# Token blocks of twice 460 or 462 columns instead of twice 384 in the middle and last stage of an attention and gated feed-forward kernel

## The chip, the cores and the metric

The kernel runs on one core of one Trainium2 chip. The time is that of one launch on the device, in microseconds (us). The profile names the engines of the core as PE (TensorE, the matrix engine), PEld (its weight loads, which overlap the matmuls), DVE (VectorE), ACT (ScalarE), POOL (GpSimd) and SP (SyncE, which issues all transfers here). Names such as L615 are lines of the kernel before.

## The reference

Sliding-window attention with a linear bias over 8 batches, 8 heads and 576 positions of width 64, and then a gated feed-forward layer over the 4608 tokens, 512 wide with 1536 hidden units:

```python
scores = scale * np.matmul(q, k.transpose(0, 1, 3, 2))
mask = (rel >= 0) & (rel < window)                       # window 128
scores = np.where(mask, scores + bias[None], -1000000000.0)
attn = softmax(scores)
x = np.matmul(attn, v) as (4608, 512)
gate = 1.0 / (1.0 + np.exp(-(x @ w_gate)))
val = x @ w_val
return (gate * val @ w_out)
```

## The kernel before

**Stages.** The first stage does the attention of 32 units (batch and pair of heads), writes x to DRAM (`xs`), and beside it `gates1` makes the hidden units of the first four chunks of 128 (`FC1`) for nine blocks of 512 tokens (L533). The middle stage, `gates2`, makes the other eight chunks of hidden units for six blocks of 768 tokens (L615), each block as two halves of N2 = 384 columns. The last stage, `results`, multiplies by `w_out` for the same six blocks (L728). Hidden units pass through DRAM in between (`hs`): `spill` stores them and `results` loads them again.

**Seven products.** Middle and last stage treat a block as a matrix of 2 x 2 parts (the two token halves by the two halves of the contraction) and form its product with the weights from seven products of sums and differences of the parts instead of eight of the parts themselves. `mix` (L659) and, in `results`, `add` (L699) form these sums on DVE; `parts` splits each into a high and a low part in a reduced format (ACT or DVE casts, L179 or L180; DVE subtracts, L188). Each product then takes three matmuls for every 128 rows of the contraction: high by high, high by low, low by high. One chunk of a block in the middle stage is 7 products x 2 x 3 = 42 matmuls of 384 columns, a block 336. A block of the last stage is 7 products x 2 output tiles x 6 pieces of the contraction x 3 = 252 matmuls of 384 columns. Each matmul has its own weights, so each has a weight load.

**Buffers.** The seven split sums of a block of the middle stage stand in three tiles, cxA (products 0, 3, 4), cxB (1, 5, 2) and cxC (6), which exist once: the next block's sum is written when the last chunk's product with the old one has been read. In the last stage the six rows of chunks of a product come in two pieces of HC = 3 chunks (1152 columns), split into seven places in turn: hF, which is memory of its own, two each in h0 and h1, which take over the memory of cxA and cxB, and two in h2, where the raw weights were. The weights of the last stage (wos0 to wos5) take over the memory of those of the middle stage (w2s0 to w2s5).

**Order.** Nothing is issued as the code is written: a planner (`Graph.order`) gives each operation a cost (for a group of matmuls, N / 2400 + 0.0133 us each) and lists them by the time at which it expects them to start. Each engine then runs its own list in order, with waits for what an operation reads. SP's queue is such a list too: loads of `xr` (x for the middle stage), `hq` and `hr` (hidden units), stores of `hs` and `out`. `follow` and `close` are entries without work that say which buffers take over which. `spill` cuts stores where a block of 512 tokens of the first stage crosses an edge between the later blocks.

## Time and profile before

| what | value |
|---|---|
| runs of before | 1019.53 us median of 3 (1019.47 to 1019.97) |
| the profiled execution | 1020.78 us, its span 1019.1 us |
| matmuls L533 / L615 / L728 | 864 / 2016 / 1512 |
| attention's last matmuls | about 303 us from the start |
| first matmul of the middle stage | 401.7 us |
| first matmul of the last stage | 751.5 us |
| last activation | 1015.2 us |

The profile is one execution. Its span is 1.7 us shorter than the time of that execution, and that time is 1.25 us above the median of the runs. A row of a group gives the number of instructions behind "x", then busy time in us and the mean duration in ns, then the idle time of the engine before them and what ended it. In the timeline a row is a run of like instructions: start, length, engine, line, operation, number. Matmuls overlap in the records: each is recorded with 334 ns while the next one starts about 173 ns later, so the spacing of starts says what a matmul costs, not its duration.

### The profile page before, as it was taken

To read this page: it belongs to the slowest core of one execution; us is meant where nothing else is said; L and a number is where in the kernel's file an instruction comes from. 1 tells how busy PE (TensorE), PEld (TensorE's weight loads), DVE (VectorE), ACT (ScalarE), POOL (GpSimd) and SP (SyncE) were. 2 spreads that over 40 slices of the span, in tenths; PEclk is the share of its full clock that TensorE was granted. 3 is DMA by queue.
4 is the path that set the end of the run, shared out by engine and by line. 5 is a ranking of instruction groups with operands and counts; after the bars stand their busy time and mean duration, and the time that the engine had idled before them with its cause. 6 is when DMAs were issued, how large, how long until landed. Compare 5 with 4: busy or idle time off the path is not lost.

```text
span 1019.1 us, 19617 instructions
## 1 busy us (share of the span) xinstructions
PE 1001.0 (98%) x7038; PEld 908.0 (89%) x7038; DVE 795.8 (78%) x2039; ACT 494.1 (48%) x1342; POOL 111.1 (11%) x211
## 2 busy tenths in 40 slices
PE   9899899999999999999999999999999999999998
PEld 7667677777777778999999999999999999999998
DVE  8999888888868887978473745547898988989881
ACT  6998777777864333454343433435364422212220
POOL 2333343333320000000000000000010000000000
PEclk9999899999999999999999999999999999999999
DMA  8776765646436554676231221313635364353401
GB/s 288 262 236 207 225 213 194 235 158 234 142 115 187 169 176 155 203 247 211 74 110 62 75 96 47 124 47 113 233 96 199 107 196 143 129 163 113 151 24 62
DMA packets 94129, 158.56 MB, mean 156 GB/s; under 512 B 8784, under 2 KB 69584, under 8 KB 94032
## 3 DMA queue, kind: packets, MB, share of 16 engines
q1 hardware_dynamic: 94032, 157.32, 46.8%
q8 instruction: 55, 0.90, 0.4%
q14 instruction: 42, 0.34, 0.1%
HBM read 106.95 MB, written 50.33 MB: 154 GB/s over the span
## 4 chain that ended last, share of the span: by engine, by line
PE 70%; DVE 15%; ACT 8%; issue 3%; DMA 3%; SPq 0%; ACTq 0%; DVEq 0%
PE mm L615 33%; PE mm L728 25%; PE mm L533 7%; ACT pb L390 5%; DVE mm L375 4%; DVE pb L387 2%; DVE work L273 2%; DVE pb L411 1%; DVE x L188 1%; ACT pb L410 1%; DVE st L405 1%; PE mm L415 1%; DMA work<-in_moe_w_val_dram 1%; PE mm L352 1%; DMA work<-in_moe_w_gate_dram 1%
## 5 line engine op out<-in xcount | busy, mean ns | idle before, releaser
L533 PE MATMUL mm<-x,w 128*128 128x512 f32 x864 | 222.9, 402 | 4.3 <-DVE x L188 3.1
L728 PE MATMUL mm<-h,wos 128*128 128x384 f32 x1296 | 226.9, 334 | 0.1
L728 PEld LDWEIGHTS mm<-h,wos 128*128 128x128 f32 x1296 | 224.8, 188 | 0.4 <-DVE h L188 0.4
L533 PEld LDWEIGHTS mm<-x,w 128*128 128x128 f32 x864 | 155.0, 188 | 45.4 <-issue 7.6
L390 ACT ACTIVATE pb<-pb,st 128x128 f32<-128x128 f32 x288 | 112.7, 394 | 39.6 <-DVE st L387 39.3
L426 POOL TENSOR_SCALAR_AFFINE_SELECT pt<-both 128x384 f32<-128x384 f32 x192 | 100.3, 546 | 193.1 <-ACT both L179 163.6
L615 PE MATMUL mm<-cxA,w2s 128*128 128x384 f32 x648 | 120.9, 334 | 0.0
L615 PE MATMUL mm<-cxB,w2s 128*128 128x384 f32 x648 | 119.6, 334 | 0.0
L615 PEld LDWEIGHTS mm<-cxA,w2s 128*128 128x128 f32 x648 | 113.2, 188 | 0.1
L615 PEld LDWEIGHTS mm<-cxB,w2s 128*128 128x128 f32 x648 | 113.0, 188 | 0.0
L622 DVE TENSOR_TENSOR mm<-mm,ring 128x384 f32<-128x384 f32 x96 | 53.7, 563 | 75.4 <-PE mm L615 72.5
L179 ACT COPY ring<-mm 128x384 f32<-128x384 f32 x144 | 69.0, 479 | 78.5 <-PE mm L615 74.9
L626 ACT ACTIVATE sg<-mm 128x384 f32<-128x384 f32 x96 | 47.2, 491 | 115.2 <-PE mm L615 65.1
L188 DVE TENSOR_TENSOR h<-hr,h 128x1152 fp32r<-128x1152 f32 x66 | 88.7, 1354 | 4.4 <-ACT h L179 1.2
L740 ACT ACTIVATE ring<-mm 128x384 f32<-128x384 f32 x48 | 23.6, 492 | 103.1 <-PE mm L728 103.1
L387 DVE CUSTOM_DVE_ANT_0 pb<-mm,relm 128x128 f32<-128x128 f32 x288 | 68.5, 285 | 1.7
L415 PE MATMUL mm<-ident,pb 128*128 128x128 f32 x288 | 52.8, 289 | 7.5 <-ACT both L179 4.1
L179 ACT CAST h<-hr 128x1152 fp32r<-128x1152 f32 x30 | 34.6, 1161 | 50.3 <-PE mm L728 31.2
L375 DVE COPY_PREDICATED mm<-swap,mm 64x128 f32<-64x128 int32 x216 | 55.2, 294 | 4.7 <-PE mm L362 1.2
L410 ACT ACTIVATE pb<-pb,st 128x128 f32<-128x128 f32 x157 | 54.0, 394 | 8.7 <-DVE st L407 8.5
L415 PEld LDWEIGHTS mm<-ident,pb 128*128 128x128 f32 x288 | 32.9, 141 | 27.9 <-ACT both L179 10.3
L187 POOL TENSOR_TENSOR work<-work 128x256 f32<-128x256 f32 x6 | 5.9, 992 | 446.8 <-ACT sg L626 429.9
(97 smaller groups left out, 1440.1 us busy)
## 6 DMA issues: line engine op xcount, KB each, us to landing
hs<-ring SPq DMA_DIRECT2D x120, 192.0 KB, 1.9
hr<-hs SPq DMA_DIRECT2D x36, 576.0 KB, 4.9
kr<-in_k_dram SPq DMA_DIRECT2D x31, 576.0 KB, 4.5
qr<-in_q_dram SPq DMA_DIRECT2D x31, 320.0 KB, 4.8
vr<-in_v_dram SPq DMA_DIRECT2D x32, 288.0 KB, 3.5
xs<-xt SPq DMA_DIRECT2D x32, 288.0 KB, 2.9
out_dram<-ring SPq DMA_DIRECT2D x48, 192.0 KB, 1.9
xr<-xs SPq DMA_DIRECT2D x10, 768.0 KB, 5.5
```

Source lines behind the costliest of these rows:

```text
L179: g.add("ACT", act_cost(n, psum), lambda: nc.scalar.copy(out(), src()), reads, writes, want, release=release, ways=[("DVE", dve_cost(n, ps ...
L188: g.add("DVE", dve_cost(n, psum, True), lambda: nc.vector.tensor_tensor(out(), a(), b(), op=ALU.subtract), reads, writes, want, port=not p ...
L375: g.add("DVE", dve_cost(2 * D, psum=True), lambda b=b, col=col, to=to, of=of: nc.vector.copy_predicated(sp[b][col, :, to:to + D], swap[col ...
L387: g.add("DVE", 0.21, lambda: nc.vector.tensor_tensor_reduce(pb()[:, e], sp[j // 2][:, j % 2, first:first + P], relm[u.p][:, w], op0=ALU.ad ...
L390: g.add("ACT", 0.39, lambda: nc.scalar.activation(pb()[:, e], pb()[:, e], AF.Exp, bias=st()[:, e:e + 1], scale=-1.0, accum_out=st()[:, 3 + ...
L410: g.add("ACT", 0.3, lambda args=args: nc.scalar.mul(*args()), [(kst, 6)], [(kpb, e)], want, ways=[("DVE", 0.16, True, lambda args=args: nc ...
L415: nc.tensor.transpose(tp[:, e], pb()[:, e], ident)
L426: nc.gpsimd.affine_select(pt(u)[:, f0:f0 + 2 * n - 1:2, :], both(), [[0, n], step], cmp, 0.0, base=0, channel_multiplier=mult)
L533: nc.tensor.matmul(mm[s], w1(kind, wi)[:, i, c * P:(c + 1) * P], x1(x)[:, c, :], start=(k == 0 and c == 0), stop=(k == 2 and c == KC - 1))
L615: nc.tensor.matmul(mm[b][:, 0:N2], w2t(i, wp)[:, wk, c * P:(c + 1) * P], combo(k, xp)[:, c], start=(start and c == 0 and j == 0), stop=(c ...
L622: g.add("DVE", dve_cost(N2, psum=True), lambda: nc.vector.tensor_tensor(o(), bk(b)(), a(), op=ALU.add), [("mm", b), *reads] if okeys else ...
L728: nc.tensor.matmul(mm[banks_[i]][:, 0:N2], wot(e * HC + c, wp)[:, k, i * P:(i + 1) * P], hcombo(s, xp)[:, c], start=(start and e == c == j ...
```

## The change

The 4608 tokens are cut into five blocks instead of six, each of two halves: two blocks with halves of 462 columns and three with halves of 460 (2 x 2 x 462 + 3 x 2 x 460 = 4608). A table of edges takes the place of multiples of 384 where stores and loads are cut. In the last stage a piece is two chunks instead of three (twice 462 columns, 924 in all), and there are nine places instead of seven: the seven sums' own places of the middle stage, one each, and two in the memory of the raw weights. hF is gone. cxA and cxC move from the general pool to the one that opens when the attention's memory is given back, so their first sums must wait for that.

```diff
-N2 = 384
-NT2 = NT // (2 * N2)
-HC = NFC // 4
-NRING, NRING1, NHC = 10, 4, 7
+HALVES = (462, 462, 460, 460, 460)
+N2, NT2 = max(HALVES), len(HALVES)
+EDGE = [2 * sum(HALVES[:b // 2]) + b % 2 * HALVES[b // 2] for b in range(2 * NT2)] + [NT]
+HC = NFC // 6
+NRING, NRING1, NHC = 10, 4, 9
...
-            b = a // N2
-            e = min((b + 1) * N2, t0 + n)
+            b = max(b for b in range(2 * NT2) if EDGE[b] <= a)
+            e = min(EDGE[b + 1], t0 + n)
...
-        return T(moe, f"c{grp}", [P, 1 if grp == "xC" else 3, 2, 2, N2], F32R, tag=grp)[:, j, part_]
+        return T(moe if grp == "xB" else pools["w2"], f"c{grp}", [P, 1 if grp == "xC" else 3, 2, 2, N2], F32R, tag=grp)[:, j, part_]
...
-        t0 = t * 2 * N2
+        N, t0 = HALVES[t], EDGE[2 * t]
...
-                            nc.tensor.matmul(mm[b][:, 0:N2], w2t(i, wp)[:, wk, c * P:(c + 1) * P], combo(k, xp)[:, c],
+                            nc.tensor.matmul(mm[b][:, 0:N], w2t(i, wp)[:, wk, c * P:(c + 1) * P], combo(k, xp)[:, c, 0:N],
...
     def hcombo(s, part_):
-        if s == 0:
-            return T(pools["w2"], "hF", [P, 2, HC, N2], F32R)[:, part_]
-        return T(moe, f"h{(s - 1) // 2}", [P, 2, 2, HC, N2], F32R, tag=("xA", "xB", "xW")[(s - 1) // 2])[:, (s - 1) % 2, part_]
+        if s < len(ORDER):
+            return combo(ORDER[s], part_)
+        return T(moe, "hw", [P, 2, 2, HC, N2], F32R, tag="xW")[:, s - len(ORDER), part_]
...
-            for e in range(2):
-                move(lambda h=h, k=k, e=e: hquad(h, k)[:, halves[e]], lambda h=h, k=k, e=e: hs[k][2 * t + h][halves[e]].rearrange("c p t -> p c t"),
+            for e in range(3):
+                move(lambda h=h, k=k, e=e: hquad(h, k)[:, third[e], 0:N], lambda h=h, k=k, e=e: hs[k][2 * t + h][third[e]].rearrange("c p t -> p c t"),
...
-        slots = {(k, e): (2 * n + e) % NHC for n, k in enumerate(ORDER) for e in range(2)}
-        m = HC * N2
+        slots = {(k, e): (3 * n + e) % NHC for n, k in enumerate(ORDER) for e in range(3)}
+        m = HC * N
...
-    g.add("PY", 0.0, close, [], touched + ["w2pool"], FIRST)
+    g.add("PY", 0.0, close, [], touched + ["w2pool"] + [k for c in (0, 3, 4, 6) for k in both_("xc", c)], FIRST)
...
-    for s0, ks in ((1, (0, 3, 4)), (3, (1, 5, 2))):
-        follow([k for c in ks for k in both_("xc", c)], both_("hc", s0) + both_("hc", s0 + 1))
-    follow([("wraw", s) for s in range(NRAW)] + [("wbits", s) for s in range(2)] + [("tt", j) for j in range(2)], both_("hc", 5) + both_("hc", 6))
+    for s0, c in enumerate(ORDER):
+        follow(both_("xc", c), both_("hc", s0))
+    follow([("wraw", s) for s in range(NRAW)] + [("wbits", s) for s in range(2)] + [("tt", j) for j in range(2)], both_("hc", 7) + both_("hc", 8))
```

The rest of the diff puts N for N2 where a width is meant. PE's list is the same as before up to the last two blocks of 512 tokens of the first stage; SP's differs earlier, in where stores are cut. Three places show how the lists differ later on. In the changed kernel some lines have moved by one (L616 is L615 of before, L189 is L188, L623 is L622, L631 is L630, L700 is L699); x6 stands for six matmuls in a row.

PE's list where the last stage begins, before. Groups from L615 belong to the last chunk of the middle stage, in which cxA, cxB and cxC are the split sums; groups from L728 belong to the first block of the last stage, hF and h0 being places of pieces and wos0 to wos5 the weights of the chunks:

```order
L615 MATMUL mm5_153<-cxA_4697,w2s5_4522 128x384 x6
L615 MATMUL mm7_155<-cxA_4697,w2s5_4522 128x384 x6
L615 MATMUL mm5_153<-cxA_4697,w2s5_4522 128x384 x6
L615 MATMUL mm6_154<-cxB_4801,w2s5_4522 128x384 x6
L615 MATMUL mm5_153<-cxB_4801,w2s5_4522 128x384 x6
L615 MATMUL mm7_155<-cxB_4801,w2s5_4522 128x384 x6
L728 MATMUL mm0_148<-hF_7238,wos0_7333 128x384 x3
L728 MATMUL mm0_148<-hF_7238,wos1_7411 128x384 x3
L728 MATMUL mm0_148<-hF_7238,wos2_7465 128x384 x3
L615 MATMUL mm5_153<-cxC_4719,w2s5_4522 128x384 x6
L728 MATMUL mm1_149<-hF_7238,wos0_7333 128x384 x3
```

The same place of the changed kernel:

```order
L616 MATMUL mm5_149<-cxA_4697,w2s5_4514 128x460 x6
L616 MATMUL mm7_151<-cxA_4697,w2s5_4514 128x460 x6
L616 MATMUL mm6_150<-cxB_4797,w2s5_4514 128x460 x6
L616 MATMUL mm5_149<-cxA_4697,w2s5_4514 128x460 x6
L616 MATMUL mm7_151<-cxB_4797,w2s5_4514 128x460 x6
L616 MATMUL mm5_149<-cxB_4797,w2s5_4514 128x460 x6
L728 MATMUL mm0_144<-cxA_4697,wos0_6881 128x462 x3
L728 MATMUL mm0_144<-cxA_4697,wos1_6952 128x462 x3
L728 MATMUL mm1_145<-cxA_4697,wos0_6881 128x462 x3
L728 MATMUL mm1_145<-cxA_4697,wos1_6952 128x462 x3
L616 MATMUL mm5_149<-cxC_4724,w2s5_4514 128x460 x6
L728 MATMUL mm0_144<-cxA_4697,wos2_7007 128x462 x3
```

The first piece of the last stage is read from cxA, in the place of the sum that the last chunk's first group has read just before, instead of from hF.

DVE's list at the same place, before. `hq0` and `hr` are the loaded hidden units, L188 rows into h0 finish a piece, L622 and L630 are work on the last chunk's results, and rows into wos5 finish the last weights:

```order
L622 TENSOR_TENSOR mm6_154<-mm6_154,ring_76 128x384
L622 TENSOR_TENSOR ring_76<-mm5_153,ring_76 128x384
L622 TENSOR_TENSOR mm7_155<-mm7_155,ring_76 128x384
L188 TENSOR_TENSOR h0_7619<-hq0_7202,h0_7619 128x1152
L630 SCALAR_TENSOR_TENSOR ring_76<-sg0_882,mm7_155 128x384
L188 TENSOR_TENSOR h0_7619<-hr_7280,h0_7619 128x1152
L630 SCALAR_TENSOR_TENSOR ring_76<-sg1_892,ring_76 128x384
L188 TENSOR_TENSOR wos5_7674<-work_193,wos5_7674 128x256
L188 TENSOR_TENSOR wos5_7674<-work_193,wos5_7674 128x1536
```

The same place of the changed kernel:

```order
L623 TENSOR_TENSOR mm6_150<-mm6_150,ring_76 128x460
L189 TENSOR_TENSOR cxA_4697<-hq0_6751,cxA_4697 128x924 x2
L623 TENSOR_TENSOR mm7_151<-mm7_151,ring_76 128x460
L189 TENSOR_TENSOR cxA_4697<-hq0_6751,cxA_4697 128x924
L623 TENSOR_TENSOR ring_76<-mm5_149,ring_76 128x460
L631 SCALAR_TENSOR_TENSOR ring_76<-sg0_878,mm7_151 128x460
L189 TENSOR_TENSOR cxB_4797<-hr_6817,cxB_4797 128x924 x3
L631 SCALAR_TENSOR_TENSOR ring_76<-sg1_888,ring_76 128x460
L189 TENSOR_TENSOR wos5_7229<-work_189,wos5_7229 128x256
L700 TENSOR_TENSOR hr_6817<-hr_6817,hq0_6751 128x924
L189 TENSOR_TENSOR wos5_7229<-work_189,wos5_7229 128x1536
```

Six pieces of 924 columns stand ahead of wos5's first row instead of two pieces of 1152.

PE's list where the second block of the middle stage ends and the third begins, before (w67 holds the weights of chunks 6 and 7, the last of a block, w2s0 and w2s1 those of chunks 0 and 1):

```order
L615 MATMUL mm7_155<-cxB_4801,w67_4787 128x384 x6
L615 MATMUL mm0_148<-cxA_4697,w2s0_4163 128x384 x6
L615 MATMUL mm5_153<-cxC_4719,w67_4787 128x384 x6
L615 MATMUL mm2_150<-cxA_4697,w2s0_4163 128x384 x6
L615 MATMUL mm0_148<-cxA_4697,w2s0_4163 128x384 x6
L615 MATMUL mm1_149<-cxB_4801,w2s0_4163 128x384 x6
L615 MATMUL mm3_151<-cxA_4697,w2s1_4215 128x384 x6
L615 MATMUL mm2_150<-cxB_4801,w2s0_4163 128x384 x6
```

The same place of the changed kernel, where the new block's first row (of 460 columns) follows the old block's last one:

```order
L616 MATMUL mm7_151<-cxB_4797,w67_4783 128x462 x6
L616 MATMUL mm5_149<-cxC_4724,w67_4783 128x462 x6
L616 MATMUL mm0_144<-cxA_4697,w2s0_4159 128x460 x6
L616 MATMUL mm2_146<-cxA_4697,w2s0_4159 128x460 x6
L616 MATMUL mm0_144<-cxA_4697,w2s0_4159 128x460 x6
L616 MATMUL mm1_145<-cxB_4797,w2s0_4159 128x460 x6
L616 MATMUL mm3_147<-cxA_4697,w2s1_4211 128x460 x6
L616 MATMUL mm5_149<-cxA_4697,w2s1_4211 128x460 x6
L616 MATMUL mm2_146<-cxB_4797,w2s0_4159 128x460 x6
```

The new block's second cxB group now comes two groups of cxA later instead of one, with the old block's cxC ahead of all of them.

More of the change, by code (lines that the diff above doesn't have):

```diff
@@ L226, in attention_gated_ffn @@
     xs = [dram.tile([KC, P, S], F32, name=f"xs{b}") for b in range(B)]
-    hs = [[dram.tile([NFC // 2, P, N2], F32, name=f"hs{k}_{b}") for b in range(NT // N2)] for k in range(2)]
+    hs = [[dram.tile([NFC // 2, P, HALVES[b // 2]], F32, name=f"hs{k}_{b}") for b in range(2 * NT2)] for k in range(2)]
     wod = [dram.tile([P, DM], F32, name=f"wod{f}") for f in range(NFC)]
@@ L606, in chunk @@
             sa, su, sp_ = scratch(), scratch(), scratch()
-            a1, u2, p5 = (lambda s=s: ring2(s) for s in (sa, su, sp_))
-            sg = [lambda h=h: sgate(h)[:, 0:N2] for h in range(2)]
-            bk = lambda b: (lambda: mm[b][:, 0:N2])
+            a1, u2, p5 = (lambda s=s: ring2(s)[:, 0:N] for s in (sa, su, sp_))
+            sg = [lambda h=h: sgate(h)[:, 0:N] for h in range(2)]
+            bk = lambda b: (lambda: mm[b][:, 0:N])
             def product(k, b, start, wk):
@@ L619, in product @@
                       [("mm", b)], 1.0e6)
             def total(o, b, a, reads, writes, okeys):
-                g.add("DVE", dve_cost(N2, psum=True), lambda: nc.vector.tensor_tensor(o(), bk(b)(), a(), op=ALU.add),
+                g.add("DVE", dve_cost(N, psum=True), lambda: nc.vector.tensor_tensor(o(), bk(b)(), a(), op=ALU.add),
                       [("mm", b), *reads] if okeys else reads, writes, F)
             def gate(b, h):
-                g.add("ACT", act_cost(N2, psum=True), lambda: nc.scalar.activation(sg[h](), bk(b)(), AF.Tanh, scale=0.5),
+                g.add("ACT", act_cost(N, psum=True), lambda: nc.scalar.activation(sg[h](), bk(b)(), AF.Tanh, scale=0.5),
@@ L634, in chunk @@
             ka, ku, kp = (("rg", s) for s in (sa, su, sp_))
             product(0, bx, True, 0)
[L636 removed]
+            copy(a1, bk(bx), N, [("mm", bx)], [ka], F, psum=True)
             product(3, bz, True, 3)
[L638 removed]
+            copy(p5, bk(bz), N, [("mm", bz)], [kp], F, psum=True)
             product(4, bx, False, 4)
[L640 removed]
+            copy(u2, bk(bx), N, [("mm", bx)], [ku], F, psum=True)
@@ L703, in results @@
         some = {}
-        bk = lambda b: (lambda: mm[b][:, 0:N2])
+        bk = lambda b: (lambda: mm[b][:, 0:N])
         def product(k, banks_, start):
-            for e in range(2):
-                x, y = (lambda a, b: (lambda: hquad(a, b)[:, halves[e]]))(0, 0), None
-                v = lambda a, b, e=e: (lambda: hquad(a, b)[:, halves[e]])
+            for e in range(3):
+                v = lambda a, b, e=e: (lambda: hquad(a, b)[:, third[e], 0:N])
                 q = lambda a, b: hk[a, b, e]
@@ L723, in product, with six @@
                         banks_.append(bank())
-                    def nine(i=i, e=e, s=s):
+                    def six(i=i, e=e, s=s):
                         for c in range(HC):
                             for j, (xp, wp) in enumerate(((0, 0), (0, 1), (1, 0))):
-                                nc.tensor.matmul(mm[banks_[i]][:, 0:N2], wot(e * HC + c, wp)[:, k, i * P:(i + 1) * P], hcombo(s, xp)[:, c],
-                                                 start=(start and e == c == j == 0), stop=(e == 1 and c == HC - 1 and j == 2),
+                                nc.tensor.matmul(mm[banks_[i]][:, 0:N], wot(e * HC + c, wp)[:, k, i * P:(i + 1) * P], hcombo(s, xp)[:, c, 0:N],
+                                                 start=(start and e == c == j == 0), stop=(e == 2 and c == HC - 1 and j == 2),
                                                  skip_group_check=True)
                     wa = 0 if k < 1 else 1
-                    g.add("PE", 3 * HC * (N2 / 2400 + 0.0133), nine,
+                    g.add("PE", 3 * HC * (N / 2400 + 0.0133), six,
                           [("hc", s, 0), ("hc", s, 1)] + [("wo", e * HC + c, p, wa) for c in range(HC) for p in range(2)],
@@ L739, in keep @@
             b = banks_[i]
-            g.add("ACT", act_cost(N2, psum=True), lambda: nc.scalar.mul(ring2(s), bk(b)(), 0.5), [("mm", b)], [("rg", s)], F)
+            g.add("ACT", act_cost(N, psum=True), lambda: nc.scalar.mul(ring2(s)[:, 0:N], bk(b)(), 0.5), [("mm", b)], [("rg", s)], F)
         def total(name, banks_, i):
             s, b = some[name, i], banks_[i]
-            g.add("DVE", dve_cost(N2, psum=True), lambda: nc.vector.scalar_tensor_tensor(
-                ring2(s), bk(b)(), 0.5, ring2(s), op0=ALU.mult, op1=ALU.add), [("mm", b)], [("rg", s)], F)
+            g.add("DVE", dve_cost(N, psum=True), lambda: nc.vector.scalar_tensor_tensor(
+                ring2(s)[:, 0:N], bk(b)(), 0.5, ring2(s)[:, 0:N], op0=ALU.mult, op1=ALU.add), [("mm", b)], [("rg", s)], F)
         def store(name, i, h, d):
```

53 lines of the change are left out of this document (25 added, 28 removed).

## The prediction

> **What bounds the kernel now.** The page comes first: its span, the busy time by engine and the clock that PE was granted in 40 slices. Then the busy time in three stretches that I cut at the stages: the end of the first stage after attention, the middle stage, the last stage (columns: stretch, PE, PEld, DVE, ACT, POOL with instructions in brackets, granted clock, share of the transfer engines, GB/s).
>
> ```profile
> span 1019.1 us, 19617 instructions
> PE 1001.0 (98%) x7038; PEld 908.0 (89%) x7038; DVE 795.8 (78%) x2039; ACT 494.1 (48%) x1342; POOL 111.1 (11%) x211
> PEclk9999899999999999999999999999999999999999
> 303.00:402.00 99.00, 97.36 (x434) 78.83 (x429) 79.32 (x136) 34.30 (x57) 0.00 (x0) 1.00 0.54 176
> 402.00:756.00 354.00, 353.64 (x2036) 352.85 (x2034) 239.47 (x398) 152.16 (x293) 5.88 (x6) 1.00 0.37 124
> 756.00:1016.00 260.00, 259.05 (x1493) 258.59 (x1492) 215.76 (x207) 68.99 (x89) 0.00 (x0) 1.00 0.40 128
> ```
>
> PE lacks 0.4 us of 354 in the middle stage; most of the 0.95 missing in the last stretch lies behind the last matmul. The clock is full in all three. A busy PE need not be a PE without waits, so the chain of waits is next (start, length, engine, what, how many), and then the timeline, for the spacing of matmuls.
>
> ```profile
> 401.89 35.57 PE mm L615 x204
> 450.35 298.17 PE mm L615 x1716
> 756.26 258.92 PE mm L728 x1492
> ...
> 382.68 1.52 PE L533 MATMUL mm<-x,w 128*128 128x512 f32 x6
> 382.68 15.57 PE L533 MATMUL mm<-x,w 128*128 128x512 f32 x68
> 401.72 6.43 PE L615 MATMUL mm<-cxA,w2s 128*128 128x384 f32 x36
> ...
> 865.24 18.88 PE L728 MATMUL mm<-h,wos 128*128 128x384 f32 x108
> 883.96 1.20 PE L728 MATMUL mm<-hF,wos 128*128 128x384 f32 x6
> ```
>
> From 401.9 us to the end the chain is matmul behind matmul but for 13 us from 437 (401.89 + 35.57) and 8 from 748, and there PE was busy too. So in both stages that the change touches, the end is set by number of matmuls times spacing. A group of 108 starts at 865.24 and the next group at 883.96: 18.72 / 108 = **173.3 ns** for 384 columns. The two rows at 382.68 are one run cut at two places: (15.57 - 1.52) / (68 - 6) = **226.6 ns** for 512. Between them: (226.6 - 173.3) / 128 = 0.416 ns a column, and 173.3 - 384 x 0.416 = **13.4 ns** for each matmul whatever its width.
>
> **The main term.** Before, 6 x (336 + 252) = 3528 matmuls x 173.3 = 611.4 us; as a check, 401.7 to 1015.2 is 613.5. After, 5 x 588 = 2940, of which 1176 have 462 columns (173.3 + 78 x 0.416 = 205.8) and 1764 have 460 (204.9): 242.0 + 361.4 = 603.4. The columns in all are the same, since 12 x 384 = 4 x 462 + 6 x 460; what goes are 588 fixed parts, 588 x 13.4 = **-7.9 us**. All of it is on the path as long as PE stays full.
>
> One rule speaks against this. The Trainium skill, "TensorE: Matmul & The Clock Gate", section "Back-to-back issue gap", gives N / 2.4 + 2.5 ns at full clock, which is 162.5 and 215.8 ns here; the rows have 173.3 and 226.6, 11 ns more at both widths. By that rule the gain would be 588 x 2.5 = 1.5 us, an estimate from the page; the rows decide, and they put 13 ns on each matmul.
>
> **What has to hide.** DVE and ACT work the same columns in fewer, wider operations in the middle stage and in more, narrower ones in the last. The groups by form from 404 us on, and a stretch of exactly one block of the last stage:
>
> ```profile
> L188 DVE TENSOR_TENSOR h<-hr,h 128x1152 fp32r<-128x1152 f32 x66 | 88.7, 1354 | 4.4 <-ACT h L179 1.2
> L744 DVE SCALAR_TENSOR_TENSOR ring<-mm,ring 128x384 f32<-128x384 f32 x36 | 19.9, 552 | 17.8 <-PE mm L728 17.7
> L188 DVE TENSOR_TENSOR cxB<-xr,cxB 128x768 fp32r<-128x768 f32 x18 | 17.1, 951 | 0.0
> L179 ACT CAST h<-hr 128x1152 fp32r<-128x1152 f32 x30 | 34.6, 1161 | 50.3 <-PE mm L728 31.2 <-DVE hr L699 17.9 <-DVE wos L188 1.2
> L179 ACT CAST cxB<-xr 128x768 fp32r<-128x768 f32 x18 | 15.2, 842 | 1.8 <-PE mm L615 1.5 <-DVE xr L659 0.2
> L180 DVE CAST h<-hr 128x1152 fp32r<-128x1152 f32 x36 | 27.3, 759 | 12.6 <-PE mm L728 12.0
> ...
> 840.00:883.68 43.68, 43.68 (x254) 43.68 (x253) 38.76 (x38) 9.76 (x13) 0.00 (x0) 1.00 0.50 156
> ```
>
> Between 768 and 1152 columns a two-input DVE operation grows by (1354 - 951) / 384 = 1.05 ns a column, so 924 take 1.11 us; an ACT cast 0.97, a DVE cast (759 x 924 / 1152) 0.61. Blocks of the last stage now last 252 x 205 = 51.7 us. DVE's list has 21 subtractions, 12 sums, 13 casts and 6 totals (552 + 78 x 1.05 = 0.63) for a steady block: 33 x 1.11 + 13 x 0.61 + 6 x 0.63 = 48.3 us, counted without the overlap of neighbours. Counted so, the 14 subtractions, 8 sums, 9 casts and 6 totals of before are 22 x 1.354 + 9 x 0.759 + 6 x 0.552 = 39.9, where the stretch shows 38.76 of 43.7; in the same ratio 48.3 become 46.9. So 91% of a block against 89%: still below PE, and DVE's idle time before totals and casts in these rows is waiting for PE. The nine places hold 9 x 12 x 205 ns = 22.1 us of matmuls, the seven 7 x 18 x 173 = 21.8: the same lead. I take 0.
>
> SP issues 12 loads of hidden units a block instead of 8, each two thirds by 1.2 as large; its list has 426 rows instead of 435, since stores get fewer.
>
> ```profile
> hr<-hs SPq DMA_DIRECT2D x36, 576.0 KB, 4.9
> ```
>
> At 4.9 us from issue to landing, and under half the transfer engines' time in use (0.40 above), a load can be late by most of the 22 us that the places hold before PE sees it. I take 0 here too.
>
> **The joints**, where leads are short: the end of the first stage, the edges between blocks of the middle stage, the hand-over to the last stage, and the end.
>
> ```profile
> L533 PE MATMUL mm<-x,w 128*128 128x512 f32 x420 | 97.1, 391 | 1.6 <-DVE x L188 0.8 <-ACT sg L543 0.5 <-ACT x L179 0.3
> 304.44 0.32 SPq L184 DMA_DIRECT2D xs<-xt  x1
> 387.64 0.56 DVE L180 CAST cxA<-xr 128x768 fp32r<-128x768 f32 x1 [1.61 <-DMA xr<-xs]
> ...
> 523.04 0.95 DVE L188 TENSOR_TENSOR cxB<-xr,cxB 128x768 fp32r<-128x768 f32 x1
> 524.41 1.20 PE L615 MATMUL mm<-cxB,w2s 128*128 128x384 f32 x6
> ...
> 706.43 1.36 DVE L188 TENSOR_TENSOR hF<-hq,hF 128x1152 fp32r<-128x1152 f32 x1
> 751.47 1.72 PE L728 MATMUL mm<-hF,wos 128*128 128x384 f32 x9
> 752.57 1.90 DVE L188 TENSOR_TENSOR h<-hq,h 128x1152 fp32r<-128x1152 f32 x1
> 755.63 19.29 PE L728 MATMUL mm<-h,wos 128*128 128x384 f32 x108
> ...
> 1015.20 0.49 ACT L740 ACTIVATE ring<-mm 128x384 f32<-128x384 f32 x1 [1.07 <-PE mm L728]
> ```
>
> First stage: PE waited 1.6 us in its last 98 us. The lists there change only in order, so this can vanish or double: -1.6 to +1.6, I take 0. The new wait of cxA and cxC for attention's memory costs nothing: attention's last store is issued at 304.44, the first cast into cxA starts at 387.64, and 83 us lie between. Loads of `xr` are cut into 17 pieces instead of 16, one of them four columns wide; they are issued a block ahead, more than 50 us.
>
> Block edges: the tightest piece, cxB for product 5, is ready at 523.99 and read at 524.41, a lead of 0.42 us. In the changed list the group waits behind one more group (1.23 us), and the DVE operations ahead of it are wider by 0.08 to 0.16 us each, some eight of them: the lead stays between 0 and 1 us. If it fails it costs up to 0.5 us at each of four edges: 0 to +2, I take 0, the end at which every edge of before lies.
>
> Hand-over: before, the first piece was ready at 707.79, 44 us before its use. Now its place is free only when the last chunk's first group is through. From there PE has five more groups (5 x 1.23 = 6.2 us). In that time ACT has a copy of a result and the cast (0.97), and DVE a total and the subtraction (1.11), behind the subtraction of the weights before (1536 columns, 1.354 + 384 x 1.05 = 1.76): about 4.4 us from the place being free, my estimate, so a lead of some 1.8 us, where before the second piece had 1.16 (754.47 to 755.63). All of PE would wait behind a late piece. The last weights, wos5, come behind six pieces on DVE: their first user starts 3.7 us after the last cxC group (one piece and half of another, 18 matmuls), and I estimate them ready 2.9 after it (the third cxB piece until 2.0, a gating 0.55, their own row 0.35). Bounds 0 to +1, I take +0.1.
>
> End: the last activation and the store are wider by 20%: 0.49 x 0.2, and as much for the store: +0.1 or +0.2, I take +0.1.
>
> Sum: -7.9 + 0.2 = -7.7, from 1020.78 to 1013.1 for an execution like the profiled one, and from the median 1019.53 to **1011.8 us**. A difference under 0.2%, 2 us, is about what a measurement of this kernel cannot tell from no change.
>
> **The rivals.**
> (1) The joints leak: two or more of the leads fail, all bounds together 1.6 + 2 + 1 = 4.6 us, 1013.5 to 1016.5. For it: leads of 0.42 and 1.16 us. Against it: PE had no gap of note at any edge, and the matmuls that cover grow with what they cover.
> (2) The fixed part does not go with the number of matmuls: if a matmul's time went in proportion to its columns, of which there are as many as before, 611.4 us would stay and the time be 1018 to 1019.5. Against it: 512 columns would then take 231.1, and the rows show 226.6. The skill's 2.5 ns leads to about the same time.
> (3) Slower: PE handles columns in steps, which 384 and 512, both multiples of 128, cannot show. In steps of 32, 460 and 462 cost as 480: 213.3 ns, 2940 x 213.3 = 627.0, +15.6, **1035 us**; in steps of 16, as 464 (206.6), 607.5, 1015.6. It decides at the place where a spacing of 611.4 / 2940 = 208.0 ns is passed. No row is for or against it.
> (4) The last stage starves: DVE is at 46.9 of 51.7 us by my count. If it needed 52.7 (12% more, say because two rows of 460 columns in places of 462 cost more than one flat row), each of five blocks would be longer by 1 us: 1017. Against it: ACT is used for 9.76 us of 43.68 and could take casts.
>
> **How the numbers follow.** Forecast (1010.5 to 1013.5) 0.74, joints 0.13, proportional 0.03, steps 0.05 (most of it slower), starving 0.03, and 0.02 below 1010.5, should the first stage's waits vanish. The range 1010.3 to 1015.8 takes the forecast, the bound of the first stage below it and most of the joints, about 0.84. Faster by over 0.2%: forecast, joints, the part below, half of the rest, 0.90; within 0.2%: 0.05; slower 0.05.
>
> **What would show it.** Spacing of 205.8 and 204.9 ns, PE busy in all but 1 us from its first 462-column matmul to the last, and some 603.5 us between them. Above 208 ns, steps; right spacing and a longer stretch, waits of PE at the four edges or where the last stage begins, with the rows that ended them. If the first 400 us differ by more than 2 us, my view of the first stage is wrong.

## The result, and the profile after

| kernel | median us | runs | ratio to before (95%) |
|---|---|---|---|
| before | 1019.75 (1019.47 to 1020.12) | 4 | |
| after | 1026.14 (1025.41 to 1028.44) | 4 | 1.0066 [1.0049, 1.0084] |

The change makes the kernel slower: by 0.66% in the ratio, by 6.4 us between the medians. Predicted were 1011.8 us. The profiled execution of the changed kernel took 1025.58 us. The page of the changed kernel gives its span, the engines' busy time and the granted clock:

```profile
span 1022.7 us, 18305 instructions
PE 1005.1 (98%) x6450; PEld 848.5 (83%) x6450; DVE 790.2 (77%) x2018; ACT 493.4 (48%) x1303; POOL 114.1 (11%) x213
PEclk9999999999999999999999999999999999999999
```

PE has the 588 matmuls less that were forecast (6450 for 7038), at full clock, and is busy for 4.1 us more. Fewer matmuls, more time: either gaps that a busy PE hides, or each one costs more. Here are the busy times in the middle and the last stage (columns as in the prediction):

```profile
402.00:752.00 350.00, 350.00 (x1668) 313.63 (x1667) 228.31 (x342) 141.57 (x242) 8.76 (x8) 1.00 0.37 126
752.00:1014.00 262.00, 262.00 (x1249) 235.14 (x1250) 219.95 (x242) 76.99 (x99) 0.00 (x0) 1.00 0.39 123
```

And the chain of waits from the end of the first stage on:

```profile
401.72 351.63 PE mm L616 x1674
753.36 2.52 PE mm L728 x12
755.88 1.27 PE mm L616 x6
757.14 261.97 PE mm L728 x1248
1019.13 0.55 ACT ring L740
```

PE is busy for all of both stretches, and the chain is matmul behind matmul without one piece of DVE, ACT or a transfer, which before had held 13 us near 437 and 8 near 748. So nothing makes PE wait. The cost is in the spacing: 1248 matmuls in 261.97 us are **209.9 ns** each, and 755.88 + 1.27 + 261.97 - 401.72 gives 617.4 us for the two stages, where 603.5 had been forecast. By the same count before had 756.26 + 258.92 - 401.89 = 613.3. The timeline of the changed kernel says the same over a few matmuls:

```profile
422.99 3.95 PE L616 MATMUL mm<-cxB,w2s 128*128 128x462 f32 x18
426.77 1.43 PE L616 MATMUL mm<-cxC,w2s 128*128 128x462 f32 x6
```

From 422.99 to 426.77 are 18 matmuls of 462 columns, 210.0 ns each; the straight line of the prediction has 205.8. Two groups of the changed kernel, by form:

```profile
L534 PE MATMUL mm<-x,w 128*128 128x512 f32 x864 | 225.5, 405 | 3.2 <-DVE x L189 2.4 <-ACT sg L544 0.5 <-ACT x L180 0.3
L616 PE MATMUL mm<-cxB,w2s 128*128 128x460 f32 x324 | 71.6, 372 | 0.0
```

And two of before, for comparison:

```profile
L728 PE MATMUL mm<-h,wos 128*128 128x384 f32 x1296 | 226.9, 334 | 0.1
L533 PE MATMUL mm<-x,w 128*128 128x512 f32 x864 | 222.9, 402 | 4.3 <-DVE x L188 3.1 <-ACT sg L543 0.6 <-ACT x L179 0.6
```

A mean duration grows with the spacing, so it is a second reading of it: 334 ns at 384 columns and 402 at 512 would put 460 at 374 if the 402 were free of waits; later rows show 389 for a 512-column matmul that waits for nothing, and by that 460 should have 367 and has 372. It is the weaker reading: in experiment 5 a mean moves by 2 ns where the spacing stays. The L534 row is a second thing that nobody had touched: the 512-column matmuls of the first stage, the same instructions as before, have a mean of 405 instead of 402. Taken from the starts of matmuls in groups of six without a wait, their spacing is 233.3 ns for 226.7 before. The stage ended within 0.2 us of before all the same (the first matmul of the middle stage starts at 401.56 us in the timeline, at 401.72 before); it has waits for other engines that may take this up, which is not shown.

The bytes where rows and weights start were the first suspect. A row of 462 columns is 1848 bytes, so in the changed kernel rows start at all multiples of 8 bytes, odd ones too, and the memory behind cxB moves to 32 bytes off a multiple of 64: all weights with it.

### The profile page after: what moved, and what is told of

It is laid out like the page before. It is cut to its first block, busy times and chain, and to the rows that moved or that the text cites. A ratio compares the mean times of both kernels' runs of the same rounds, so it can differ in the third digit from the quotient of the medians.

```text
span 1022.7 us, 18305 instructions
## 1 busy us (share of the span) xinstructions
PE 1005.1 (98%) x6450; PEld 848.5 (83%) x6450; DVE 790.2 (77%) x2018; ACT 493.4 (48%) x1303; POOL 114.1 (11%) x213
## 4 chain that ended last, share of the span: by engine, by line
PE 78%; DVE 12%; ACT 7%; issue 2%; DMA 0%; POOL 0%; ACTq 0%; DVEq 0%; POOLq 0%
PE mm L616 35%; PE mm L728 26%; PE mm L534 13%; ACT pb L391 4%; DVE mm L376 3%; DVE pb L388 2%; DVE pb L412 1%; PE mm L416 1%; DVE st L406 1%; PE mm L477 1%; DVE x L189 1%; PE mm L363 1%; DVE xt L489 1%; ACT pb L411 1%; PE mm L353 1%
## 5 line engine op out<-in xcount | busy, mean ns | idle before, releaser
L534 PE MATMUL mm<-x,w 128*128 128x512 f32 x864 | 225.5, 405 | 3.2 <-DVE x L189 2.4
L534 PEld LDWEIGHTS mm<-x,w 128*128 128x128 f32 x864 | 155.3, 188 | 46.4 <-issue 7.6
L616 PE MATMUL mm<-cxA,w2s 128*128 128x460 f32 (+1 forms) x540 | 120.1, 372 | 0.0
L616 PE MATMUL mm<-cxB,w2s 128*128 128x460 f32 (+1 forms) x540 | 119.6, 372 | 0.0
L728 PE MATMUL mm<-cxA,wos 128*128 128x460 f32 (+1 forms) x540 | 115.3, 372 | 0.0
L623 DVE TENSOR_TENSOR mm<-mm,ring 128x460 f32<-128x460 f32 (+1 forms) x80 | 51.3, 643 | 82.2 <-PE mm L616 82.1
L616 PEld LDWEIGHTS mm<-cxB,w2s 128*128 128x128 f32 x540 | 101.6, 188 | 12.0 <-ACT ring L180 0.3
L616 PEld LDWEIGHTS mm<-cxA,w2s 128*128 128x128 f32 x540 | 101.6, 188 | 11.8
L728 PEld LDWEIGHTS mm<-cxA,wos 128*128 128x128 f32 x540 | 101.7, 188 | 11.5
L180 ACT COPY ring<-mm 128x460 f32<-128x460 f32 (+1 forms) x120 | 65.4, 545 | 86.2 <-PE mm L616 84.4
L627 ACT ACTIVATE sg<-mm 128x460 f32<-128x460 f32 (+1 forms) x80 | 44.6, 557 | 116.6 <-PE mm L616 73.0
L728 PE MATMUL mm<-cxB,wos 128*128 128x460 f32 (+1 forms) x360 | 77.5, 372 | 0.0
L728 PEld LDWEIGHTS mm<-cxB,wos 128*128 128x128 f32 x360 | 67.8, 188 | 7.9
L740 ACT ACTIVATE ring<-mm 128x460 f32<-128x460 f32 (+1 forms) x40 | 22.3, 557 | 87.0 <-PE mm L728 87.0
L188 POOL TENSOR_TENSOR work<-work 128x256 f32<-128x256 f32 x8 | 8.8, 1100 | 439.8 <-DMA work<-wod 311.2
```

The source lines that it names most:

```text
L180: g.add("ACT", act_cost(n, psum), lambda: nc.scalar.copy(out(), src()), reads, writes, want, release=release, ways=[("DVE", dve_cost(n, ps ...
L534: nc.tensor.matmul(mm[s], w1(kind, wi)[:, i, c * P:(c + 1) * P], x1(x)[:, c, :], start=(k == 0 and c == 0), stop=(k == 2 and c == KC - 1))
L616: nc.tensor.matmul(mm[b][:, 0:N], w2t(i, wp)[:, wk, c * P:(c + 1) * P], combo(k, xp)[:, c, 0:N], start=(start and c == 0 and j == 0), stop ...
L623: g.add("DVE", dve_cost(N, psum=True), lambda: nc.vector.tensor_tensor(o(), bk(b)(), a(), op=ALU.add), [("mm", b), *reads] if okeys else r ...
L627: g.add("ACT", act_cost(N, psum=True), lambda: nc.scalar.activation(sg[h](), bk(b)(), AF.Tanh, scale=0.5), [("mm", b)], [("sg", h)], F)
L728: nc.tensor.matmul(mm[banks_[i]][:, 0:N], wot(e * HC + c, wp)[:, k, i * P:(i + 1) * P], hcombo(s, xp)[:, c, 0:N], start=(start and e == c ...
```

## The experiments

In tables and text, "spacing" is worked out from the recorded starts: in the kernels over groups of six matmuls in a row without a wait, in the runs with matmuls alone from the 7th start to the 43rd of a section of 48, divided by 36. "Excess" is the spacing less 0.4167 ns a column and 13.33 ns, the line through 384 (173.3) and 512 columns (226.7). Beside the first four, before had 1019.66 us.

**1. Rows of 464 columns' length, everything at multiples of 64 bytes.**

```diff
-N2, NT2 = max(HALVES), len(HALVES)
+N2, NT2 = 464, len(HALVES)
```

> The changed kernel with the same blocks of twice 462 or 460 columns, but the split sums, ring, x and hidden units kept in rows of 464 columns (1856 bytes) instead of 462 (1848), so that every row of columns and every tile of weights starts at a multiple of 64 bytes. Theory W (the weights' addresses): in the changed kernel all weights start 32 bytes past a multiple of 64, and each matmul pays for it, 6.7 ns in the first stage (233.3 against 226.7 ns) and 4.6 in the later ones (210.0 against the 205.4 of the prediction); here spacing 205 to 206 ns, 226.7 at 512 columns, 1011 to 1013 us. Theory R (the addresses of the rows of columns): the later stages as under W, the first stage not explained. Theory S (the width itself costs 210 ns, in steps or in another way): spacing stays 210 ns and the time 1025 to 1027.

1023.0 us (1021.79 to 1023.72), 1.003 [1.0019, 1.0040]. From its chain of waits:

```profile
400.19 351.15 PE mm L616 x1674
...
755.13 261.46 PE mm L728 x1248
```

From its groups by form:

```profile
L534 PE MATMUL mm<-x,w 128*128 128x512 f32 x864 | 222.4, 402 | 3.5 <-DVE x L189 2.6 <-ACT x L180 0.8 <-ACT sg L544 0.2
L616 PE MATMUL mm<-cxB,w2s 128*128 128x460 f32 x324 | 71.5, 372 | 0.0
```

The 512-column matmuls are back at 402 (spacing 226.7), and the middle stage begins 1.5 us earlier. The 460-column ones stay at 372, with a spacing of 209.1 and 210.4 ns for 460 and 462. Addresses at multiples of 64 bytes mend the first stage and not the two others, so theories W and R, which had 205 to 206 ns there, fall.

**2. Weights at multiples of 64 bytes, rows still 1848 bytes apart.**

```diff
-    x1 = lambda part_: T(moe, "x1", [P, 9 * DM], F32R, tag="xB")[:, part_ * KC * NB:(part_ + 1) * KC * NB].rearrange("p (c t) -> p c t", c=KC)
+    x1 = lambda part_: T(moe, "x1", [P, max(9 * DM, 12 * N2) + 8], F32R, tag="xB")[:, part_ * KC * NB:(part_ + 1) * KC * NB].rearrange("p (c t) -> p c t", c=KC)
```

> The changed kernel with 32 bytes of padding behind the tile of x and cxB, so that all weights start at a multiple of 64 bytes; the rows of columns stay 1848 bytes apart and start at all multiples of 8 within 64 bytes. Theory W (the weights' addresses): first stage 226.7 ns, later stages 205 to 206 ns, 1011 to 1013 us. Theory R (the rows' addresses): 210 ns in the later stages, 1025 to 1027 us. Theory S (the width): 210 ns, 1025 to 1027 us.

1024.31 us (1023.57 to 1024.97), 1.0045 [1.0028, 1.0062]. 512 columns: 228.9 ns; 460: 209.5 to 209.8; 462: 210.5 to 211.1. The later stages stay where they were. The first stage lies between the two values seen. Its rows and weights start 22208 bytes apart here, 64 less than a multiple of 256, and in experiment 1 22272, a multiple of 256.

**3. Rows of 464 columns' length, weights 32 bytes off.** Both edits.

> Rows of 464 columns as in the run with all rows at multiples of 64 bytes, and 32 bytes of padding that put all weights, and with them cxA and cxC, 32 bytes past a multiple of 64; rows of cxB stay at multiples of 64. Theory W (the weights' addresses): 233 ns at 512 columns in the first stage, 210 to 212 ns for cxA and cxB alike, 1025 to 1032 us. Theory R (the rows' addresses): 205 to 206 ns for cxB, more for cxA and cxC, 1011 to 1020 us. Theory S (the width): 210 ns for all, 1025 to 1027 us.

1025.71 us (1025.42 to 1026.23), 1.0057 [1.0042, 1.0072]. 512 columns: 233.3 ns; 460: 209.6; 462: 210.2. The middle stage begins at 403.78 us, 3.6 later than in experiment 1; 864 x 6.7 = 5.8 us are the most that the 6.7 ns at 512 columns can cost before it.

**4. Six blocks of twice 384 columns, weights 32 bytes off.** The changed kernel with its pieces in thirds over nine places, but the old widths, and the edit of experiment 2.

```diff
-HALVES = (462, 462, 460, 460, 460)
+HALVES = (384,) * 6
```

> The changed kernel's code with six blocks of twice 384 columns (pieces still in thirds over nine places), and 32 bytes of padding that put all weights, cxA and cxC 32 bytes past a multiple of 64; cxB stays at multiples of 64. Theory W (the weights' addresses): 178 to 180 ns instead of 173.3 for cxA and cxB alike, 3528 x 4.6 to 6.7 = 16 to 23 us more, 1036 to 1043 us. Theory R (the rows' addresses): 173.3 ns for cxB, more for cxA and cxC, 1020 to 1033 us. Theory S (the width): 173.3 ns throughout, 1019 to 1021 us.

1023.26 us (1022.69 to 1024.22), 1.0034 [1.0021, 1.0048]. 512 columns: 233.3 ns, the middle stage from 402.79 us; 384: 174.2 ns in the middle stage and 174.0 in the last, for 173.8 and 173.3 in experiment 6, which lacks only the 32 bytes. The 32 bytes that cost 6.7 ns at 512 cost under 1 ns at 384: the width decides how much an address can cost. In all they cost 2.8 us against experiment 6, 1.7 of them before the middle stage; theory S, with 1019 to 1021 us, had left out the first stage's share.

**5. Matmuls alone, 26 widths.** No other engine works beside them, at a granted clock of 1.00:

```python
for r in range(ROUNDS):                                  # 16
    for j, (xp, wp) in enumerate(((0, 0), (0, 1), (1, 0))):
        nc.tensor.matmul(b[:, 0:n], w[:, (2 * r + wp) % 8], x[:, xp, at:at + n],
                         start=(r == 0 and j == 0), stop=(r == ROUNDS - 1 and j == 2), skip_group_check=True)
```

> Leaves the whole computation out: only matmuls on random data, 48 in a row for each of 26 widths from 256 to 512 columns (the order of weights and rows as in the kernel's three-fold products), first with rows and weights at multiples of 64 B, then weights 32 B off, then rows 32 B off, and some widths with rows 8 B off; the output is zeros. No wait stands between them, so the spacing is that of TensorE alone. The straight line of the prediction gives 0.416 ns a column + 13.4: 173.3 at 384, 199.9 at 448, 204.9 at 460, 205.8 at 462, 206.6 at 464, 213.3 at 480, 226.6 at 512. Theory S (the width itself costs): at 460 to 464 about 209 to 210 ns with everything at multiples of 64 B; if by steps of 32 columns, 480 would be on the line and 460 as much as 480 (213.3, already too much by the runs so far); if by a fixed price on every width that is no multiple of 64, 448 and 512 lie on the line and all others 4 to 5 ns above it; if it is a bend, the excess grows smoothly from 384 to the middle and falls to 512. Theory N (nothing in the width, something that the kernel does beside the matmuls, as vector engine traffic into the same memory): all widths within 1 ns of the line. Weights 32 B off: +6.7 ns at 512, 0 at 384, and the width from which it begins is read off between them.

Groups by form, xa and wa being the rows and weights at multiples of 64 bytes, xb and wb those 32 bytes off:

```profile
L60 PE MATMUL mm<-xa,wa 128*128 128x462 f32 x48 | 10.3, 374 | 0.0
L60 PE MATMUL mm<-xb,wa 128*128 128x462 f32 x48 | 10.1, 368 | 0.0
L60 PE MATMUL mm<-xa,wb 128*128 128x512 f32 x48 | 11.4, 396 | 0.0
L60 PE MATMUL mm<-xb,wa 128*128 128x512 f32 x48 | 11.4, 395 | 0.0
L60 PE MATMUL mm<-xa,wa 128*128 128x384 f32 x96 | 17.0, 334 | 0.0
L60 PE MATMUL mm<-xa,wb 128*128 128x384 f32 x48 | 8.5, 336 | 0.0
L60 PE MATMUL mm<-xb,wa 128*128 128x384 f32 x48 | 8.5, 336 | 0.0
```

With the same width 462, the mean goes from 374 to 368 as the rows move by 32 bytes. At 384 it goes from 334 to 336 with either move, without a change of spacing. The excess in ns, from the starts, for 16 of the widths:

| columns | all at 64 B | weights 32 B off | rows 32 B off |
|---|---|---|---|
| 320, 352, 384 | 0.0 | 0.0 | 0.0 |
| 388 | 1.7 | 5.0 | 1.7 |
| 400 | 0.0 | 3.4 | 0.0 |
| 416 | 0.0 | 3.4 | 0.0 |
| 424 | 0.0 | 3.3 | 2.1 |
| 432 | 2.2 | 6.7 | 3.3 |
| 448 | 2.8 | 4.5 | 6.7 |
| 460 | 3.9 | 1.7 | 6.1 |
| 462 | 5.7 | 5.2 | 0.8 |
| 464 | 2.2 | 6.7 | 4.5 |
| 480 | 3.3 | 6.7 | 4.5 |
| 488 | 9.0 | 3.4 | 3.3 |
| 496 | 3.3 | 6.7 | 4.5 |
| 512 | 0.0 to 0.4 | 6.7 | 6.7 |

From 320 to 384 columns the line holds to 0.1 ns, whatever the addresses. From 388 on a matmul costs up to 7 ns more, once 9, and the addresses choose how much. Theory N falls, since nothing works beside PE. Steps of 32 columns would put 480 on the line, a fixed price would put 448 there, and a bend would fall smoothly: none fits. 512 columns with everything at multiples of 64 bytes, the one wide width that before uses, is a place where the excess is nothing. So the two widths of before, from which the line was drawn, lie on it; with everything at multiples of 64 bytes only 400, 416 and 424 do too among the widths between them.

**6. Thirds over nine places alone**, with the old widths and aligned addresses: only `HALVES = (384,) * 6`.

> Six token blocks of twice 384 columns, as in the kernel before, with rows and weights at multiples of 64 B; of the change only the pieces of h in thirds over nine places stay. If the thirds cost nothing: 1019.5 to 1020.3 us, no difference from before, with 226.7 ns at 512 columns and 173.3 at 384. If the thirds cost as the 384-column kernel with weights 32 B off hinted (its vector engine stood in the chain of waits at the hand-over to the last stage): 1021 to 1023, with the idle time of TensorE before its first matmul of the last stage.

1020.42 us (1019.66 to 1021.84) beside 1019.73, 1.0009 [0.9999, 1.0018]: no difference that can be told. From its chain:

```profile
401.06 337.69 PE mm L616 x1944
...
752.10 262.10 PE mm L728 x1512
```

262.10 us by 1512 are 173.3 ns. No cost of the thirds can be told.

**7. Offsets, and shorter weight loads.** Matmuls alone again, with rows and weights moved by 8 to 128 bytes, with 64 and 32 columns of weights for 128, and with one row or one weight for two.

> Leaves the whole computation out, as the run over widths did: sections of 48 matmuls in a row on random data, output zeros. There no other engine worked, and still 388 columns and more cost 0 to 6.7 ns above the line (most often 0, 1.7, 3.3, 5.0 or 6.7 ns; 512 at multiples of 64 B nothing, 512 with rows or weights 32 B off 6.7), while 256 to 384 columns cost nothing, whatever the addresses. Two theories. K (the weight load collides: a matmul's rows are read while the next matmul's weights are loaded, and from about 388 columns on the two meet, with addresses deciding how): the excess goes to 0 to 1 ns where a weight load is shorter (64 or 32 columns of weights instead of 128), at 460, 464, 480 and 512, whatever the offset of the rows; with 128 columns it stays 2 to 7 ns and depends on the offset of the rows (8, 16, 32, 64 B) and of the weights. L (it belongs to the rows' reading alone, as a row that ends in the middle of some unit): 64 and 32 columns of weights leave the excess as it is, and offsets of the weights change nothing. Whether the same section gives the same time again (460, 462, 464, 480, 512 come twice) tells whether addresses and width fix it, or what ran before does: theory H (history) has them differ by 1 ns or more. For the kernel: an offset of rows or weights at which 460 to 464 columns cost under 1 ns above the line would bring five blocks back to 1012 to 1015 us, if H is wrong.

| excess, ns | 460 | 462 | 464 | 480 | 512 |
|---|---|---|---|---|---|
| first time / second time | 1.7 / 1.7 | 5.8 / 5.8 | 2.2 / 2.2 | 3.3 / 3.3 | 0.0 / 0.0 |
| rows + 8 B | 5.0 | 0.8 | 0.0 | 0.0 | 6.7 |
| rows + 32 B | 6.1 | 0.9 | 4.5 | 4.5 | 6.7 |
| weights + 32 B | 3.9 | 5.3 | 6.7 | 6.7 | 6.7 |
| rows and weights + 32 B | 3.9 | 5.6 | 2.2 | 3.3 | 0.0 |
| 64 columns of weights | 0.3 | | 0.0 | 3.3 | 3.3 |
| 32 columns of weights | 1.7 | | 6.7 | 0.0 | 5.0 |

History falls for a section as a whole: the same section gives the same time. L falls: moving the weights alone matters. If both move by 32 bytes, the excess at 462 to 512 is what it was with neither moved (at 460 it goes from 1.7 to 3.9, the value of experiment 5, where the distance was 256 bytes less). So at 462 to 512 columns it is the distance between rows and weights that counts; at 460 something else counts too. More of the distance counts than its last 128 bytes: with weights 128 bytes away, 464 columns go from 2.2 to 6.7. K, in the form in which it was put, falls too: with 64 and 32 columns of weights the excess moves, but does not go. Nor does it go with one row, one weight or both used all the time: with rows 32 bytes off it is then 1.7 at 460, 4.5 at 464 and 6.7 at 480 and 512 columns.

**8. The kernel's own order of rows and weights**, 16 starts of the rows, 8 bytes apart.

> Leaves the whole computation out (output zeros): sections of 48 matmuls in a row, now with the kernel's own order of weights and rows (two halves of the sum, three products each) and its distance between rows, 464 or 480 columns, at 16 starts of the rows 8 B apart from one another, the weights 128 B past a multiple of 512 as the kernel has them. In the run over offsets the excess over the line came back to 0.1 ns for the same addresses and moved between 0 and 8 ns with the distance between rows and weights, also with short weights. Theory A (the excess is fixed by the width and by where rows and weights lie to each other): there are starts at which 462 and 464 columns cost 207 ns or less, 460 at most 207, and others at 211 to 213 ns; at the start that the kernel with rows of 464 columns has (0 B), 460 and 462 come out at 209 to 211, as there. Theory B (the kernel's distances between rows mix all phases, so that the start matters no more): every start gives 209 to 211 ns for 460 to 464 columns at rows of 464, and no choice of addresses brings the five blocks under the six.

With rows 464 columns apart, 460 columns take 206.7 to 211.6 ns over the 16 starts, 209.5 on the mean; 462 take 207.9 to 212.2, 210.2 on the mean. At the start that experiment 1 has, it is 208.2 and 210.0, where the kernel showed 209.1 and 210.4. With rows 480 columns apart the means are 209.4 and 210.2, with the weights 384 bytes further on 209.4 and 209.9. Theory B is nearer, though single starts leave its 209 to 211 ns: no start tried brings both widths to the line (205.0 and 205.8). The best, 16 bytes, has 206.7 and 208.9. That phases mix, since rows come at several distances from the weights, fits but is not shown. With 512 columns in rows of 512 it is 226.7, and with 384 it is 173.3.

**9. Five blocks of the widths that lie on the line.** Three blocks of twice 512 and two of twice 384 have as many columns, 4608, and as many matmuls, 2940, as the change. Rows 512 columns apart keep one distance to all weights, but for multiples of 512 bytes. They need more memory, so the ring is smaller and the raw pieces move together (the lines that say which piece lies in which of the two buffers are left out):

```diff
-HALVES = (462, 462, 460, 460, 460)
-N2, NT2 = max(HALVES), len(HALVES)
+HALVES = (512, 512, 512, 384, 384)
+N2, NT2 = 512, len(HALVES)
...
-NRING, NRING1, NHC = 10, 4, 9
+NRING, NRING1, NHC = 6, 4, 9
...
-    hr = lambda: T(moe, "hr", [P, 3, NFC // 2, N2], F32, tag="wA")
+    hr = lambda: T(moe, "hr", [P, 16, N2], F32, tag="wA")
...
-    hq0 = lambda: T(moe, "hq0", [P, NFC // 2, N2], F32, tag="xr")
+    hq0 = lambda: T(moe, "hq0", [P, 8, N2], F32, tag="xr")
```

> Five token blocks again, as many matmuls as in the change, but with halves of 512, 512, 512, 384 and 384 columns: the two widths that cost nothing above the line in the runs over widths and over rows, with every row and weight at the same distance from a multiple of 512 B. To fit, the ring has six places instead of ten and a third of a raw quarter of h lies in the tail of the memory of the token loads. If the excess at 448 to 496 columns is the whole cause of the loss (theory S, the width with its addresses): 226.7 and 173.3 ns, 1764 x 226.7 + 1176 x 173.3 = 603.7 us of matmuls in the two later stages, and 1012 to 1014 us, with at most 2 us more where the smaller ring or the wider pieces make TensorE wait. If five blocks lose for another reason that the 210 ns only hide (theory J, joints and thirds: vector engine and transfers): PE gaps at block edges or at the hand-over, and 1018 us or more in spite of 226.7 and 173.3 ns. If wide matmuls in these stages cost more than in the first stage whatever their width (theory T): about 233 ns at 512, 1764 x 6.7 = 11.8 us more, 1024.

**1012.79 us** (1011.19 to 1013.41) beside 1019.38, 0.9930 [0.9916, 0.9944]: faster than before and than the change. From its chain of waits (L734 is L728 of the change):

```profile
401.45 328.54 PE mm L616 x1583
...
740.18 2.09 DVE wos L189
...
749.94 1.67 DVE wos L189
...
752.13 1.31 PE mm L616 x6
753.44 254.72 PE mm L734 x1242
```

From its groups by form:

```profile
L616 PE MATMUL mm<-cxB,w2s 128*128 128x512 f32 x324 | 77.2, 389 | 0.0
L734 PE MATMUL mm<-cxA,wos 128*128 128x384 f32 x216 | 38.3, 334 | 0.0
```

Its busy times about the hand-over:

```profile
728.00:754.00 26.00, 24.59 (x131) 22.41 (x130) 23.88 (x37) 15.11 (x26) 7.10 (x6) 1.00 0.26 87
```

753.44 + 254.72 - 401.45 are 606.7 us for both stages. The matmuls alone were put at 603.7. Of the other 3.0 us, 2.6 lie between 720 and 760 us, by the starts: there the chain runs over DVE for most of the 22 us from 730 to 752, and 1.4 us are PE's idle time (26.00 - 24.59). The spacing is 226.7 and 173.3 in most groups. Theories J and T fall as the cause of the loss, but once matmuls are as cheap as the line, the hand-over does cost something (here with a ring of six places).

**10. The same with a shift of 32 bytes** behind the place B. Weights, A and C move with it, B and the two spare places (hw) don't: the edit of experiment 2, with `12 * N2 + 8`.

> The same with 32 B put behind the rows' memory that the first stage and products 1, 5 and 2 use: weights and the places A and C move by 32 B, the place B and the two spare places do not. If the distance between rows and weights decides (theory D): 512 columns cost 226.7 ns where rows lie in A or C, 233.3 where they lie in B or in the spare places: 432 + 420 matmuls more by 6.7 ns, 5.7 us, and about 3 us from the first stage, which as a whole reads rows that did not move: 8 to 9 us above the run without the 32 B. If the weights' own start decides (theory W): 233.3 ns at all 512-column matmuls of these stages, 11.8 + 3 = 15 us above it. If neither counts in these stages: 226.7 everywhere, up to 3 us above. 384 columns: 173.3 in all cases.

1020.35 us (1020.01 to 1023.2), 1.0011 [1.0001, 1.0020]: 7.6 us are gone, for 32 bytes. This run separates the two readings of the addresses, since weights are 32 bytes off everywhere, but only some rows moved with them. Its timeline:

```profile
422.76 2.88 PE L616 MATMUL mm<-cxA,w2s 128*128 128x512 f32 x12
425.48 1.56 PE L616 MATMUL mm<-cxB,w2s 128*128 128x512 f32 x6
426.88 1.55 PE L616 MATMUL mm<-cxA,w2s 128*128 128x512 f32 x6
428.26 2.96 PE L616 MATMUL mm<-cxB,w2s 128*128 128x512 f32 x12
...
435.17 4.36 PE L616 MATMUL mm<-cxB,w2s 128*128 128x512 f32 x18
439.37 0.85 PE L616 MATMUL mm<-cxC,w2s 128*128 128x512 f32 x3
```

Its groups by form:

```profile
L616 PE MATMUL mm<-cxB,w2s 128*128 128x512 f32 x324 | 79.4, 396 | 0.0
L616 PE MATMUL mm<-cxA,w2s 128*128 128x512 f32 x324 | 77.4, 390 | 0.0
L734 PE MATMUL mm<-hw,wos 128*128 128x512 f32 x144 | 34.6, 396 | 0.0
```

Twelve matmuls out of cxA take 425.48 - 422.76 = 2.72 us, 226.7 ns each; eighteen out of cxB take 439.37 - 435.17 = 4.20, 233.3 each. In the means, 390 against 396. Within one kernel, with one set of weights, the rows that kept their distance to them are at or near the line and those that did not pay 6.7 ns. Theory D holds, W falls. Over all groups of six the means are 227.8 and 233.5. A quarter of the groups from A and C has 230.7, and they are those that come right behind a group from B or the spare places: 40 of 42 such groups have it, and 114 of the 116 others have less than 228 (in the rows above, 428.26 - 426.88 = 1.38 us for six). There the excess runs on for about five matmuls, so what ran just before counts as well. From 402.22 us to the end of the last matmul at 1015.08, the two stages take 612.9 us, 6.2 more than in experiment 9; D had put 5.7 there. Of the 3 us that D had for the first stage, the beginning of the middle stage shows 0.8 (402.22 for 401.45).

## Why the prediction was wrong

**What bounds the kernel: right.** The end is set by the number of matmuls times their spacing, before and after.

**The number of matmuls: right.** 2940, and no gap among them.

**The price of one matmul: wrong, and it is the whole miss.** The step that failed reads: "Between them: (226.6 - 173.3) / 128 = 0.416 ns a column", and from it 205.8 and 204.9 ns at 462 and 460. The changed kernel shows 209.9 over the last stage. 2940 x (209.9 - 205.2) = 13.8 us, and the two stages took 617.4 us where 603.5 were forecast, 13.9 more. The prediction missed the median by 14.3. The line itself is sound at the widths that it was drawn from; experiment 5 shows it to hold at 320 to 384 and at an aligned 512 and to be missed by up to 9 ns at most widths between. The fixed part of 13.4 ns is real as well: with 384 and 512 columns, experiment 9 got 1012.8 us out of the same 588 matmuls less, where 1011.8 was forecast for the change.

**Rival 3 had the right side and the wrong form.** It named the point from which it decides, 208.0 ns, and the spacing passed it. But columns are not handled in steps: steps of 32 would have given 213.3 ns and 1035 us, steps of 16 206.6. Its chance of 0.05 was too small for a number taken between two widths that are both multiples of 128, with no row in the trace of any between them. The same goes for the range, which gave the spacing no width at all, while it spent 4.6 us on the joints.

**Rival 2**, time in proportion to columns, came near the measured time by its size (208 ns) and is wrong as a mechanism: experiment 9 has fewer matmuls with the same columns and gains.

**The joints, the hand-over and the end: right, in part perhaps by luck.** The middle stage began within 0.2 us of before, no edge shows a wait, the last stage began without a gap, and the last activation took 0.55 us for 0.49. But PE was slower by 4.7 ns a matmul than forecast, which gave DVE more time everywhere; experiment 9, with matmuls at the price of the line and a smaller ring, loses 2.6 us about the hand-over, where +0.1 was forecast. **The supply of the last stage: right.** PE was busy for 262.00 of 262.00 us, and no cost of the thirds alone can be told (experiment 6). DVE's load was counted well: a stretch as long as the third block, from its first matmul to the next block's, has

```profile
860.51:913.33 52.82, 52.82 (x254) 47.52 (x252) 46.58 (x53) 12.17 (x16) 0.00 (x0) 1.00 0.46 140
```

with 46.6 us of DVE, where 46.9 had been counted.

**The first stage: its time right, its matmuls not.** That its 512-column matmuls would cost 6.7 ns more, because the new size of cxB's place moved its weights by 32 bytes, was not thought of. How much of it reaches the beginning of the middle stage differs: 3.6 us between experiments 1 and 3, 1.7 between 6 and 4, 0.8 between 9 and 10, and nothing between before and the changed kernel. Why is not shown. So the time of this stage came out as forecast with a cost in it that was not foreseen, which is luck.

**What stays open.** Why the excess begins above 384 columns, why so many of its values are near 1.7, 3.3, 5.0 or 6.7 ns, why 460 columns do not go by the distance alone, and what meets what. That rows and weights are read at once and collide would fit the distance that counts, but short weight loads and a single weight (experiment 7) did not take the excess away, so it is only argued.

## What to carry to other kernels

Before a width is changed, measure the spacing at that very width: here a line through 384 and 512 columns was 4 to 5 ns too low at 460 and 462. Equal blocks are no virtue of their own: here three of twice 512 and two of twice 384 beat five of twice 460 or 462 by 13 us with as many matmuls. And a change of one buffer's size moves all that lies behind it, so look at the spacing of matmuls that the diff does not touch. For widths above 384, the distance between rows and weights is worth measuring: at 512 columns a multiple of 256 bytes was free here.
